# Start-up constants, early loads, transposes, filler matmuls and the last store rearranged in a fused window-attention and SwiGLU kernel

## The chip, the cores and the metric

The kernel runs on one core of one Trainium2 chip. The metric is the device time of one execution in microseconds. The median of 10 runs of the kernel before is 250.42 us (250.11 to 251.44). Five engines have their own instruction queues, each worked off in order: TensorE (PE, with its weight loads shown as PEld), VectorE (DVE), ScalarE (ACT), GpSimd (POOL) and SyncE (SP).

## The reference

Attention over a sliding window of 128 keys plus four sink tokens, for 4 batches of 8 heads with 768 positions of 64 dimensions; its output, as 3072 rows of 512, goes through RMS normalisation and a SwiGLU feed-forward network (FFN) with 1536 hidden columns.

```python
scores = scale * np.matmul(q, k.transpose(0, 1, 3, 2))
keep = is_sink | in_window            # pos < 4, or 0 <= i - j < 128
scores = np.where(keep, scores, -1000000000.0)
a = np.exp(scores - max); a = a / (sum(a) + 1e-09)
x = np.matmul(a, v)                   # to 3072 x 512
xn = x / sqrt(mean(x * x) + 1e-06) * rms_g
g = xn @ w_gate
out = (g * sigmoid(g) * (xn @ w_val)) @ w_out
```

## The kernel before, in words

**Tiling.** A block is 128 positions of one batch with all eight heads; there are 24 blocks, six a batch, numbered 0 to 23. The loop over blocks makes, for each: q and k transposed to put the head dimension on the partitions; scores of its 128 keys against its own and the next block's queries (64-row matmuls, two heads at once); exponentials on ACT; a causal and a window triangle; the attention-value product with a column of ones that gives the denominators; division; RMS normalisation; and a transpose of the normalised x. From the third block of a batch on, the sink keys enter with their own small matmuls (`ss`, `vs`). Four blocks make a group; the FFN works on six groups. An FFN unit is a `g` and a `v` part of 16 matmuls of 128 columns in group 0 (one block and four tiles of hidden columns at a time), eight of 256 in groups 1 and 2, four of 512 after that. Then the output projection `o` takes 12 matmuls for each block of 128 rows; ACT evicts it, SP stores it.

**Who sets the order.** No engine decides anything at run time. Every operation is given to a planner (class Plan) with the engines that may do it, an estimated duration, what it needs and gives, a priority and the PSUM banks it takes or drops. `Plan.run` repeatedly picks the operation that can start first, by its own estimates of engines, of DMA rings and of the eight PSUM banks, with the priority to break ties. The order it finds is then written out and is what the in-order engine queues contain. A change of any cost or priority can therefore reorder all engines.

**Loads.** q, k, v and the weights come in fp32 and are cast to bf16 on their way by DMAs that POOL issues (L327, L331, L374, L380), in the order of the string LOADS, at most eight under way (DEPTH). Only q of block 0 comes as fp32 over ACT's DMA queue, and ACT casts it (L319, L323). The gain of the normalisation, `grow`, comes over SP and is spread over the partitions by a one-row fp32 matmul `gb` (L395).

**Constants.** DVE sets tiles to a value, POOL's affine selects cut them: the identity (L253), two bias triangles (L260, L265), two mask triangles (the same lines), `sel` (L288) and `headm` (L297, L302). Blocks 0 to 2 get their triangles from PE, which adds the biases to the scores with four 512-column matmuls (L434, PE_MASKS); blocks 3 to 11 get them from DVE, by a product with the masks (L482), and later blocks from POOL (L487, L492), except the first block of a batch, which stays on DVE.

**Transposes.** q, k (L412) and x (L575) of blocks 0 to 9 are transposed by PE into PSUM and copied out by DVE or ACT (L419, L581). From block 10 on, SP issues DMA transposes from SBUF to SBUF (L426, L587); those of q and k wait for the scores of three blocks before.

**Gates.** Scores of block 8 and later wait for an FFN unit chosen by GATE_FROM and GATE_LEAD, so that attention does not run too far ahead of the FFN. SPLIT names the blocks whose scores are made in two halves, those against the own queries first.

Of the kernel before, what the change touches and what calls it, by code (L numbers as in the profile page):

```python
# [9 lines left out]
ALU = mybir.AluOpType  # L10
ACT = mybir.ActivationFunctionType
# [4 lines left out]
P = 128  # L16
# [7 lines left out]
NEG = -30000.0  # L24


class Plan:
# [21 lines left out]
    def land(self, ring, first, work):  # L49
# [3 lines left out]
        if ring == "POOL":  # L53
            r["POOL"] = max(first, r["POOL"], r["HW"]) + work
            self.loads -= 1
            return r["POOL"] + 520
# [10 lines left out]
    def run(self):  # L67
# [12 lines left out]
        while left:  # L80
# [23 lines left out]
            if e == "PE":  # L104
                busy = [(a, d) for a, d in busy if a > start - 4000]
                warm = start - free[e] < 4000 and (warm or sum(d for a, d in busy) > 2600)
                ns = ns if warm else 1.9 * ns
                if o["mode"] != mode:
                    ns, mode = ns + 110, o["mode"]
                busy.append((start, ns))  # L110
# [24 lines left out]
def kernel(  # L135
# [33 lines left out]
    F32_LOADS = ("q0",)  # L169
    POOL_AT = (0,2,6)  # L170
    DEPTH = 8
    LOADS = "k-0 v-0 qk-1 w-0-2 qkv-2 v-1 w-2-5 qkv-3 w-5-9 w-9-12 qkv-4 wo-0-6 qkv-5 wo-6-12 qkv-6 qkv-7 qkv-8"
    LOADS += "".join(f" qkv-{g}" for g in range(9, NB))
    PE_MASKS = 3
    POOL_MASK_FROM = 12
    X_DMA_FROM = 10
    QK_DMA_FROM = 10
    LD = 16
    GATE_FROM = 8
    GATE_LEAD = 2  # L180
    T_LEAD = 3
    SPLIT = (0,)
    CHUNKS = (4,2,2)
    GB_PRIO = -1200
# [35 lines left out]
    headm = const.tile([P, H], BF16, name="headm")  # L220
# [27 lines left out]
    dve(480, lambda: nc.vector.memset(masks, 1.0), gives=["masks0"], prio=-40)  # L248
    dve(70, lambda: nc.vector.memset(sel, 0.0), gives=["sel0"], prio=-39)
    dve(70, lambda: nc.vector.memset(headm, 1.0), gives=["headm0"], prio=-38)  # L250
# [7 lines left out]
    def triangle(t, fill, i):  # L258
        if i == 0:
            nc.gpsimd.affine_select(  # L260
                out=t, in_=t, compare_op=ALU.is_ge,
                fill=fill, base=0, pattern=[[1, P]], channel_multiplier=-1,
            )
        else:
            nc.gpsimd.affine_select(  # L265
                out=t, in_=t, compare_op=ALU.is_ge,
                fill=fill, base=-1, pattern=[[-1, P]], channel_multiplier=1,
            )
# [5 lines left out]
    def spread_masks():  # L274
        nc.vector.tensor_copy(out=masks[:, 0, :, :], in_=masks[:, 1, :, :])
        nc.vector.memset(masks[0:NS, 0, :, :], 1.0)

    pool(270, make_ident, ["id0"], ["ident"], -89.2 + POOL_AT[0])
    for i in range(2):
        pool(270, lambda i=i: triangle(bias[:, i, :], NEG, i), ["bias0"],  # L280
             [("bias", i)], -89.1 + POOL_AT[1] + i / 100)
# [598 lines left out]
```

## Time and profile before

| what | us |
|---|---|
| median of 10 runs | 250.42 |
| the profiled execution, own time | 250.14 |
| its span, first to last instruction | 248.4 |
| PE busy | 238.2 (96%) |
| PE weight loads busy | 148.7 (60%) |
| DVE busy | 177.7 (72%) |
| ACT busy | 133.0 (54%) |
| POOL busy | 95.2 (38%) |
| first real matmul starts | 3.97 |
| last matmul ends | 244.64 |
| issue to landing, fp32 q of block 0 | 3.0 |
| issue to landing, a 256 KB store, median | 2.2 |

Times in the profile are microseconds from the first instruction, so the span is shorter than the execution's own time by what lies around it. Matmuls overlap one another, so a busy time of PE does not tell how fast it runs; the chain of the work that ended last gives start-to-start prices. A line such as L452 is the line of the kernel. In the changed kernel most lines stand a few numbers lower or higher: L452 becomes L455, L412 L415, L434 L437, L752 L755, L785 L788.

### The profile page before, as it was taken

Reading aid. Unit: us, or ns where it says so; the run is one execution under the profiler, and the core shown is the slowest. Engines: PE = TensorE matmul, PEld = TensorE weight load, DVE = VectorE, ACT = ScalarE, POOL = GpSimd, SP = SyncE. Lnnn points to the kernel's source line nnn. Section 1 sums busy time; section 2 is a strip of 40 time slices with the busy share of each in tenths; the row PEclk is TensorE's granted clock in tenths of the full one; section 3 lists DMA queues with packets and bytes.
Section 4 is the critical chain, followed back from the end, with each engine's and each line's share of the span. In section 5 each row is a group of like instructions: output and inputs, shape, how many; then the busy total and the mean of one; then the engine's idle time right before and its main releaser. Section 6 shows DMA issues by size and latency. Waiting matters only on the chain.

```text
span 248.4 us, 5479 instructions
## 1 busy us (share of the span) xinstructions
PE 238.2 (96%) x2094; PEld 148.7 (60%) x2094; DVE 177.7 (72%) x470; ACT 133.0 (54%) x277; POOL 95.2 (38%) x129
## 2 busy tenths in 40 slices
PE   3898999999999999999999999999999999999993
PEld 1456998696689875589775445444455454444441
DVE  2376889699899996599986089997279993377700
ACT  3566466787937644645753545644645543333111
POOL 8996455599942589204403111020303320000000
PEclk9999999999999999999999999999999999999999
DMA  9999999999999999996222533212501102200022
GB/s 90 148 178 187 199 189 186 156 180 154 150 172 154 147 155 148 170 200 90 42 46 63 148 66 65 56 31 80 152 24 22 22 18 83 112 3 0 0 84 84
DMA packets 107003, 26.43 MB, mean 106 GB/s; under 512 B 98273, under 2 KB 103905, under 8 KB 106978
## 3 DMA queue, kind: packets, MB, share of 16 engines
q0 software_dynamic: 79632, 14.03, 75.6%
q1 hardware_dynamic: 26306, 11.81, 23.7%
q8 instruction: 16, 0.26, 0.5%
q10 hardware_dynamic: 1040, 0.26, 0.5%
q14 instruction: 9, 0.07, 0.1%
HBM read 28.31 MB, written 6.29 MB: 139 GB/s over the span
## 4 chain that ended last, share of the span: by engine, by line
PE 93%; DMA 2%; ACT 1%; DVE 1%; POOL 1%; issue 1%; POOLq 0%
PE o L785 25%; PE g L752 25%; PE v L752 25%; PE s L452 5%; PE av L516 3%; PE av L511 2%; DMA q<-in_q_dram 2%; PE ss L618 1%; PE av L501 1%; PE q L412 1%; PE x L575 1%; PE k L412 1%; PE gb L395 1%; PE s L434 1%; ACT e L465 1%
## 5 line engine op out<-in xcount | busy, mean ns | idle before, releaser
L752 PE MATMUL v<-xnt,wv 128*128 128x128 bf16 (+2 forms) x528 | 72.6, 282 | 0.2 <-DMA wv<-in_moe_w_val_dram 0.2
L752 PE MATMUL g<-xnt,wg 128*128 128x128 bf16 (+2 forms) x528 | 70.2, 282 | 0.1
L759 ACT ACTIVATE th<-g 128x512 bf16<-128x512 f32 x72 | 43.1, 602 | 43.4 <-PE g L752 43.3
L765 DVE SCALAR_TENSOR_TENSOR p<-th,g 128x512 bf16<-128x512 bf16 x72 | 48.1, 684 | 25.2 <-ACT th L759 24.9
L785 PE MATMUL o<-wo,hT 128*128 128x512 bf16 x288 | 66.1, 379 | 0.0
L752 PEld LDWEIGHTS <-wg 128*128 128x128 bf16 x528 | 43.1, 98 | 19.4 <-issue 1.6
L465 ACT ACTIVATE e<-s 128x512 bf16<-128x512 f32 (+1 forms) x100 | 48.4, 553 | 10.2 <-PE s L452 10.1
L752 PEld LDWEIGHTS <-wv 128*128 128x128 bf16 x528 | 42.4, 98 | 18.2 <-issue 1.1
L775 DVE TENSOR_TENSOR hT<-p,v 128x512 bf16<-128x512 bf16 x72 | 47.7, 682 | 1.8 <-PE v L752 0.8
L785 PEld LDWEIGHTS <-hT 128*128 128x128 bf16 x288 | 26.8, 97 | 30.1 <-issue 0.8
L487 POOL TENSOR_SCALAR_AFFINE_SELECT e<-e 128x512 bf16<-128x512 bf16 x20 | 13.9, 698 | 80.3 <-ACT e L465 54.0
L793 ACT ACTIVATE osb<-o 128x512 f32<-128x512 f32 x24 | 14.5, 603 | 26.1 <-PE o L785 25.9
L327 POOL DMA_DIRECT2D k<-in_k_dram x24 | 21.5, 896 | 10.1 <-DMA v<-in_v_dram 2.5
L327 POOL DMA_DIRECT2D q<-in_q_dram x23 | 20.6, 895 | 10.6 <-DMA wo<-in_moe_w_out_dram 3.0
L536 ACT ACTIVATE sq<-x 128x512 bf16<-128x512 bf16 x24 | 15.2, 633 | 17.0 <-DVE x L528 16.8
L331 POOL DMA_DIRECT2D v<-in_v_dram x24 | 21.5, 894 | 5.8 <-DMA q<-in_q_dram 4.7
L528 DVE TENSOR_TENSOR x<-av,rden 128x256 bf16<-128x256 f32 x48 | 20.4, 425 | 1.7
L560 DVE SCALAR_TENSOR_TENSOR xr<-x,r,gb 128x512 bf16<-128x512 bf16 x24 | 18.0, 752 | 0.9
L516 PE MATMUL av<-v,e 128*128 128x65 bf16 x192 | 17.1, 195 | 0.2
L452 PE MATMUL s<-qkT 64*128 64x256 bf16 (+1 forms) x200 | 14.5, 268 | 0.8 <-DVE qkT L419 0.5
L511 PE MATMUL av<-v,e 128*128 128x65 bf16 x160 | 14.8, 193 | 0.0
L516 PEld LDWEIGHTS <-e 128*128 128x128 bf16 x192 | 13.0, 99 | 2.0 <-ACT e L465 0.5
(68 smaller groups left out, 175.1 us busy)
## 6 DMA issues: line engine op xcount, KB each, us to landing
out_dram<-osb SPq DMA_DIRECT2D x24, 256.0 KB, 2.2
k<-in_k_dram POOLq DMA_DIRECT2D x24, 128.0 KB, 7.9
v<-in_v_dram POOLq DMA_DIRECT2D x24, 128.0 KB, 8.4
q<-in_q_dram POOLq DMA_DIRECT2D x23, 128.0 KB, 7.7
wo<-in_moe_w_out_dram POOLq DMA_DIRECT2D x2, 768.0 KB, 13.4
wg<-in_moe_w_gate_dram POOLq DMA_DIRECT2D x2, 384.0 KB, 9.3
wv<-in_moe_w_val_dram POOLq DMA_DIRECT2D x2, 384.0 KB, 10.4
wg<-in_moe_w_gate_dram POOLq DMA_DIRECT2D x1, 512.0 KB, 9.3
```

The lines of the kernel that those rows point to most:

```text
L327: nc.gpsimd.dma_start(out=T[name, g], in_=block_of(src, g))
L331: nc.gpsimd.dma_start(out=V16[b][:, t, :, 0:D], in_=block_of(v, g))
L452: nc.tensor.matmul(out=BANK[slot][:, j * 256 + n0 * P:j * 256 + n1 * P], lhsT=qkT[pr, 1, hp, t * P:(t + 1) * P], rhs=qkT[pr, 0, hp, (t + n ...
L465: nc.scalar.activation(out=T["e", g, u][:, 2 * hi:2 * hi + 2, n0:n1, :].rearrange("p x n c -> p x (n c)"), in_=ps.rearrange("p (j c) -> p ...
L511: nc.tensor.matmul(out=dest, lhsT=T["e", g - 1, u][:, x, 1, :], rhs=V16[b][:, t - 1, h, :], start=(t == 1), stop=False, skip_group_check=True,
L516: nc.tensor.matmul(out=dest, lhsT=T["e", g, u][:, x, 0, :], rhs=V16[b][:, t, h, :], start=(t == 0), stop=True, skip_group_check=True,)
L528: nc.vector.tensor_tensor(out=T["x16", g][:, 4 * u:4 * u + 4, :], in0=pvv[:, :, 0:D], in1=rden.unsqueeze(2).to_broadcast((P, 4, D)), op=AL ...
L752: nc.tensor.matmul(out=ps[:, i * n:(i + 1) * n], lhsT=w_sb[:, kt, ft * P:(ft + 1) * P], rhs=T["xnt", G][:, kt, cols], start=(kt == 0), sto ...
L759: nc.scalar.activation(out=T["th", key], in_=BANK[("g", key)], func=ACT.Tanh, scale=0.5,)
L765: nc.vector.scalar_tensor_tensor(out=T["p1", key], in0=T.pop(("th", key)), scalar=1.0, in1=BANK.pop(("g", key)), op0=ALU.add, op1=ALU.mult,)
L775: nc.vector.tensor_tensor(out=T[hk][:, i:i + n, cols], in0=T.pop(("p1", key)).rearrange("p (n c) -> p n c", n=n), in1=BANK.pop(("v", key)) ...
L785: nc.tensor.matmul(out=BANK[("o", G, tb)], lhsT=T["h", G, ft // 4][:, ft % 4, tb * P:(tb + 1) * P], rhs=wo[:, ft, :], start=(ft == 0), sto ...
```

## The change

- **Constants.** POOL makes the identity and one bias triangle. DVE makes the other bias as the complement of the first (with a fill of -32768), both masks from the biases by a comparison with zero, `sel` as a copy of identity columns and `headm` as a sum over them. POOL issues its first load before it makes the identity.
- **Loads.** q and k of block 0 and q of block 1 come as fp32 over SP; q0 and k0 are cast on ACT and q1 on DVE. `grow` comes over ACT. LOADS changes its order: smaller pieces of the gate and value weights, block 3 ahead of tiles 2 and 3, block 8 ahead of blocks 6 and 7. From block 9 on, a block's loads wait for the scores of nine blocks before.
- **Transposes** of q, k and x by DMA from block 8.
- **Masks.** PE adds the bias for blocks 0 to 3; POOL masks from block 14.
- **Gates.** Attention may run eight FFN units further ahead, from block 6; scores of blocks 1 and 2 are split too.
- **Fillers.** 20 matmuls of 128 columns on a tile of zeros, into a PSUM bank of their own, at the lowest priority: the planner puts them where PE is idle by its estimate. In the resulting order seven stand ahead of everything, the rest in ones to threes up to block 2's bias.
- **The last block.** Its output projection is made in two halves of 256 columns; ACT evicts and stores the first, DVE evicts and SP stores the second.
- **Planner.** Its estimates of early DMA transfers, of load latency and of when PE runs at full speed change.

The diff, cut to its core:

```diff
-NEG = -30000.0
+NEG = -32768.0
...
-            r["POOL"] = max(first, r["POOL"], r["HW"]) + work
+            begin = max(first, r["POOL"], r["HW"])
+            r["POOL"] = begin + (1.4 * work if begin < 8500 else work)
...
-                busy = [(a, d) for a, d in busy if a > start - 4000]
-                warm = start - free[e] < 4000 and (warm or sum(d for a, d in busy) > 2600)
-                ns = ns if warm else 1.9 * ns
+                busy = [(a, d) for a, d in busy if a > start - 3413]
+                warm = start - free[e] < 4000 and (warm or sum(d for a, d in busy) > 3000)
+                ns = ns if warm else 2 * ns
                 if o["mode"] != mode:
                     ns, mode = ns + 110, o["mode"]
-                busy.append((start, ns))
+                busy.append((start, ns if mode < 2 else 0))
...
-    F32_LOADS = ("q0",)
-    POOL_AT = (0,2,6)
+    F32_LOADS = ("qs0","ks0","qs1")
+    GROW = "ACT"
+    CAST_DVE = 1500
+    MASKS_PRIO = -5
+    POOL_AT = (0,1)
     DEPTH = 8
-    LOADS = "k-0 v-0 qk-1 w-0-2 qkv-2 v-1 w-2-5 qkv-3 w-5-9 w-9-12 qkv-4 wo-0-6 qkv-5 wo-6-12 qkv-6 qkv-7 qkv-8"
+    LOADS = "k-1 v-0 qkv-2 w-0-2 v-1 qkv-3 w-2-4 w-4-6 w-6-8 w-8-9 w-9-12 qkv-4 wo-0-6 qkv-5 wo-6-12 qkv-8 qkv-6 qkv-7"
     LOADS += "".join(f" qkv-{g}" for g in range(9, NB))
-    PE_MASKS = 3
-    POOL_MASK_FROM = 12
-    X_DMA_FROM = 10
-    QK_DMA_FROM = 10
+    PE_MASKS = 4
+    POOL_MASK_FROM = 14
+    X_DMA_FROM = 8
+    QK_DMA_FROM = 8
     LD = 16
-    GATE_FROM = 8
-    GATE_LEAD = 2
+    GATE_FROM = 6
+    LOAD_LEAD = 9
+    LEAD_FROM = 9
+    WARM = 20
+    GATE_LEAD = 10
     T_LEAD = 3
-    SPLIT = (0,)
+    SPLIT = (0,1,2)
     CHUNKS = (4,2,2)
-    GB_PRIO = -1200
+    GB_PRIO = 2000
...
+    if WARM:
+        zeros = const.tile([P, P], BF16, name="zeros")
+        dve(70, lambda: nc.vector.memset(zeros, 0.0), gives=["zeros"], prio=-99.6)
...
+    def make_bias():
+        nc.gpsimd.affine_select(
+            out=bias[:, 0, :], in_=bias[:, 0, :], compare_op=ALU.is_ge,
+            fill=NEG, base=0, pattern=[[1, P]], channel_multiplier=-1,
+        )
+    def other_bias():
+        nc.vector.tensor_scalar(
+            out=bias[:, 1, :], in0=bias[:, 0, :], scalar1=-1.0, scalar2=NEG,
+            op0=ALU.mult, op1=ALU.add,
+        )
...
+    def make_masks():
+        for i in range(2):
+            nc.vector.tensor_scalar(
+                out=masks[:, i], in0=bias, scalar1=0.0, scalar2=None, op0=ALU.is_equal,
+            )
         nc.vector.memset(masks[0:NS, 0, :, :], 1.0)
+    def make_sel():
+        nc.vector.tensor_copy(
+            out=sel[:, 0:H * NS].rearrange("p (h s) -> p h s", s=NS),
+            in_=ident[:, 0:NS].unsqueeze(1).to_broadcast((P, H, NS)),
+        )
+        nc.vector.reduce_sum(
+            out=headm, in_=ident[:, 0:H * NS].rearrange("p (h s) -> p h s", s=NS),
+            axis=mybir.AxisListType.X,
+        )
...
     pool(270, make_ident, ["id0"], ["ident"], -89.2 + POOL_AT[0])
-    for i in range(2):
-        pool(270, lambda i=i: triangle(bias[:, i, :], NEG, i), ["bias0"],
-             [("bias", i)], -89.1 + POOL_AT[1] + i / 100)
-        pool(330, lambda i=i: triangle(masks[:, 1, i, :], 0.0, i), ["masks0"],
-             [("masks1", i)], -89.1 + POOL_AT[2] + i / 100)
-    dve(220, cut_ident, ["ident"], ["idnos"], -50)
-    dve(600, spread_masks, [("masks1", 0), ("masks1", 1)], ["masks"], -20)
-
...
-    pool(200, make_sel, ["sel0"], ["sel"], -89.1 + POOL_AT[2] + 1)
-    pool(180, lambda: make_headm(0), ["headm0"], ["headm1"], -89.1 + POOL_AT[2] + 2)
-    pool(180, lambda: make_headm(1), ["headm1"], ["headm"], -89.1 + POOL_AT[2] + 3)
+    pool(270, make_bias, ["bias0"], [("bias", 0)], -89.1 + POOL_AT[1])
+    dve(130, other_bias, [("bias", 0)], [("bias", 1)], -60)
+    dve(220, cut_ident, ["ident"], ["idnos"], -59)
+    dve(700, make_masks, [("bias", 0), ("bias", 1)], ["masks"], MASKS_PRIO)
+    dve(300, make_sel, ["ident", "sel0"], ["sel", "headm"], MASKS_PRIO + 1)
...
-        n, g = name[0], int(name[1:])
-        src, first, fn = q if n == "q" else k, i % 2 == 0, load_f32
-        if first:
-            op({"ACT": (450, 1000, lambda n=n, src=src, g=g: load_f32(n, src, g, nc.scalar))},
-               (), [(n + "st", g)], -90 + i, ring="HW", work=970)
-        else:
-            sp(400, 1000, lambda n=n, src=src, g=g: load_f32(n, src, g, nc.sync),
-               (), [(n + "st", g)], -90 + i, ring="HW", work=970)
-        act(640, lambda n=n, g=g: cast(n, g, nc.scalar.copy), [(n + "st", g), "table"],
-            [(n, g)], -99)
-    sp(400, 1000, lambda: nc.sync.dma_start(
-        out=grow, in_=moe_rms_g.rearrange("(o d) -> o d", o=1)), (), ["grow"], -89.5, ring="HW", work=50)
+        n, g, e = name[0], int(name[2:]), {"s": "SP", "a": "ACT"}[name[1]]
+        src, eng = q if n == "q" else k, {"SP": nc.sync, "ACT": nc.scalar}[e]
+        op({e: (430, 1000, lambda n=n, src=src, g=g, eng=eng: load_f32(n, src, g, eng))},
+           (), [(n + "st", g)], -90 + i, ring="HW", work=970)
+        either({"DVE": (CAST_DVE, lambda n=n, g=g: cast(n, g, nc.vector.tensor_copy)),
+                "ACT": (640, lambda n=n, g=g: cast(n, g, nc.scalar.copy))},
+               [(n + "st", g), "table"], [(n, g)], -99)
+    op({GROW: (430, 1000, lambda: {"SP": nc.sync, "ACT": nc.scalar}[GROW].dma_start(
+        out=grow, in_=moe_rms_g.rearrange("(o d) -> o d", o=1)))}, (), ["grow"], -89.5,
+        ring="HW", work=50)
...
-        op({"POOL": (ns, 1720, fn)}, list(needs) + more, list(gives) + [("sw", n)], -89 + n,
+        op({"POOL": (ns, 1900, fn)}, list(needs) + more, list(gives) + [("sw", n)], -89 + n,
...
-        old = g - LD
         for n in what:
+            needs = [("s", g - LOAD_LEAD)] if g >= LEAD_FROM else []
             if n == "v":
-                sw_load(lambda g=g: load_v(g), [("v", g)], 910)
+                sw_load(lambda g=g: load_v(g), [("v", g)], 910, needs=needs)
             else:
                 src = q if n == "q" else k
+                needs += [(n + "T", g - LD)] if g >= LD else []
                 sw_load(lambda n=n, src=src, g=g: load_bf16(n, src, g), [(n, g)], 860,
-                        needs=[(n + "T", old)] if old >= 0 else [])
+                        needs=needs)
...
+    def warm(i):
+        ps = bank(("warm",)) if i == 0 else BANK[("warm",)]
+        nc.tensor.matmul(out=ps[:, 0:P], lhsT=zeros, rhs=zeros, start=True, stop=True)
+    for i in range(WARM):
+        pe(55, lambda i=i: warm(i), ["zeros"] + ([("warm", i - 1)] if i else []),
+           [("warm", i)], 1e9, takes=[("warm",)] if i == 0 else (),
+           drops=[("warm",)] if i == WARM - 1 else ())
...
+    def project_half(i):
+        ps = bank(("o", "last", i))
+        for ft in range(FTN):
+            nc.tensor.matmul(
+                out=ps[:, 0:DM // 2],
+                lhsT=T["h", NG - 1, ft // 4][:, ft % 4, GN - P:GN],
+                rhs=wo[:, ft, i * DM // 2:(i + 1) * DM // 2],
+                start=(ft == 0), stop=(ft == FTN - 1),
+            )
+    def evacuate_half(i):
+        T["last", i] = opool.tile([P, DM // 2], FP32, name=f"last{i}", bufs=1)
+        ps = BANK[("o", "last", i)][:, 0:DM // 2]
+        if i:
+            nc.vector.tensor_scalar(
+                out=T["last", i], in0=ps, scalar1=0.5, scalar2=None, op0=ALU.mult,
+            )
+        else:
+            nc.scalar.mul(T["last", i], ps, 0.5)
+    def store_half(i):
+        (nc.scalar if i == 0 else nc.sync).dma_start(
+            out=out[NB * P - P:NB * P, i * DM // 2:(i + 1) * DM // 2], in_=T["last", i],
+        )
...
-        for tb in range(GB):
+        for tb in range(GB if G < NG - 1 else GB - 1):
...
+    for i in range(2):
+        pe(12 * 109, lambda i=i: project_half(i), [("h", key) for key in mine]
+           + [("O", NG - 1, GB - 2)], [("ol", i)], 1e5 + i, takes=[("o", "last", i)])
+        (dve if i else act)(330, lambda i=i: evacuate_half(i), [("ol", i)], [("ev", i)],
+                            drops=[("o", "last", i)])
+        op({"SP" if i else "ACT": (420, 1000, lambda i=i: store_half(i))}, [("ev", i)], (),
+           ring="ST", work=440)
```

## The prediction

> **What bounds the kernel now.** I read the busy time by stretch first, because it tells where TensorE is not full. Columns: stretch in us, its length, then busy us (and instructions) of PE, weight loads, DVE, ACT and POOL, granted clock, DMA share, GB/s.
>
> ```profile
> 10.00:15.00 5.00, 5.00 (x35) 2.90 (x34) 2.99 (x13) 2.97 (x9) 4.99 (x8) 1.00 2.06 161
> 15.00:20.00 5.00, 4.37 (x59) 3.06 (x56) 2.64 (x9) 3.73 (x9) 3.87 (x6) 1.00 1.58 185
> 20.00:25.00 5.00, 4.10 (x60) 3.37 (x61) 3.38 (x10) 3.71 (x8) 3.47 (x4) 1.00 1.58 194
> 25.00:30.00 5.00, 5.00 (x96) 4.83 (x94) 4.05 (x14) 2.37 (x6) 1.92 (x3) 1.00 1.30 205
> 30.00:240.00 210.00, 209.89 (x1810) 130.04 (x1808) 161.77 (x410) 115.29 (x239) 71.91 (x92) 1.00 0.96 98
> ```
>
> From 25 us to the end PE idles for 0.1 us. So the end is the moment at which PE becomes full, plus the work left, plus the tail after the last matmul. The second view is the waits, of PE alone: every one of them lies before 25 us.
>
> ```profile
> PE s L434 <- POOL bias L265: 4.0, 1, 4.0
> PE q L412 <- DMA q<-in_q_dram: 0.6, 2, 0.3
> PE x L575 <- DVE xr L560: 0.5, 1, 0.5
> PE v L752 <- DMA wv<-in_moe_w_val_dram: 0.2, 1, 0.2
> ```
>
> A busy PE need not be a fast PE. Third, the timeline: four mask matmuls of 512 columns, the same instruction three times (start, us).
>
> ```profile
> 3.97 1.86 PE L434 MATMUL s<-bias,idnos 128*128 128x512 bf16 x4 [3.97 <-POOL bias L265]
> ...
> 12.48 1.91 PE L434 MATMUL s<-bias,ident 128*128 128x512 bf16 x4
> ...
> 16.18 1.04 PE L434 MATMUL s<-bias,ident 128*128 128x512 bf16 x4
> ```
>
> The granted clock says 1.00 throughout, but equal work costs 1.9 us before about 16 us and half of that after. Fourth, the chain that ended last gives the prices of the steps (start, us, step):
>
> ```profile
> 8.73 2.00 PE gb L395 x2
> ...
> 12.69 1.71 PE s L434 x4
> ...
> 33.64 0.22 PE q L412 x4
> ...
> 45.50 0.86 PE o L785 x4
> 46.72 0.33 PE s L452 x8
> 47.04 0.97 PE o L785 x4
> ...
> 244.64 0.60 ACT osb L793
> ```
>
> Prices at full speed: a 128-column transpose of four 0.22; four 512-column matmuls 0.86; a change into or out of the 64-row score matmuls 0.11 (0.97 less 0.86). With these I price everything PE has issued by 25.96 us, where it is full: 12 mask matmuls 2.6, ten transposes 2.2, scores of blocks 0 to 2 with their changes 2.4, sink work 0.7, gb 0.9, attention-value products 1.5, four FFN units of 0.89 make 3.6; 13.8 in all. The start therefore loses 25.96 - 13.8 = **12.1 us**, and only this, PE's later work, and the tail can change the time.
>
> **The change, part by part.**
>
> *PE's later work.* Blocks 8 and 9 lose q, k and x transposes on PE: 6 x 0.22 = -1.33. Block 3 gets its mask on PE (PE_MASKS 4): +0.86. Splitting the scores of blocks 1 and 2 adds one visit to the 64-row mode net: 2 x 0.11 = +0.22. The last block's 12 matmuls of 512 columns become 24 of 256; the trace's 256-column FFN units cost 0.87 for eight, the same per column: 0. Sum **-0.2**. Off PE, ACT and DVE lose six copies (0.59 or 0.42 each); DVE trades block 3's two masks (0.69 each) for those of block 13, which leave POOL; both are hidden under a full PE.
>
> *Tail.* From the last matmul, 244.64, to the end of the span, 248.43, is 3.8: an eviction of 0.60, a store of 256 KB that takes at best 2.0 from issue to landing, and the close. Now the last eviction is half as wide, on DVE (the 128x256 read from PSUM at L528 takes 0.43): -0.17. Half a store saves between 0 and 1.0 (all of it proportional); the issue (0.33) and the latency do not shrink, so I take -0.3. Sum **-0.45**.
>
> *Constants.* Six selects leave POOL (0.33, 0.33, 0.31, 0.29, 0.21, 0.21: 1.7 us of busy time). POOL issues the loads, but a load issued at 7.61 landed at 13.54, just 0.95 behind the one ahead of it: the transfers queue for some 6 us, so a faster POOL is worth nothing there. What counts is the very first load, issued at 1.47 and now ahead of the identity, about a microsecond earlier, and the first mask: it waits for one select and a DVE op instead of two selects behind two DMA issues, so PE starts near 2.5 instead of 3.97. DVE takes the rest, about 1 us, before its first copy at 6.73.
>
> [...] The cast of q1, fp32 SBUF to SBUF, goes to DVE now. [...] The row: POOL's issue of k at 8.74 took 0.92 beside a 0.42 DVE copy at 8.77 (PSUM source, so not quite the case), against a 0.88 median. [...]
>
> *Order of loads.* q0, k0 and q1 come as fp32 over SP (the old q0 took 2.98 from issue to landing); k0 and q1 landed at 5.27 and 8.08 before, and I expect 5 and 6.3. But the transfers ahead of the weights of the first FFN unit are about as many: before, nine 128 KB blocks' worth (q0, k0, v0, q1, k1, q2, k2, v2, v1) and ten 128 KB weight slices until wv of tiles 2 to 4 landed at 20.00; now these nine plus q3, k3, v3 (0.9 each, +2.7) but two slices of weights fewer (-1.3 to -1.6), with a start about 1 us earlier: wg near 18.7, wv near 20. The loads of blocks 9 on wait for scores nine blocks back. The wait holds up POOL's queue: the loads behind it, and last the block masks from block 14. By PE's order block 14's scores come near 107, so block 23's loads issue then instead of 98 to 100; block 14's masks come right after them and its attention-value product near 131, and block 23 is needed near 178. Covered; uncovered it would be the 2.7 us of four masks (about 0.67 each).
>
> *Fillers.* Twenty 128-column matmuls on zeros: seven while PE has nothing to do, 13 between real ones at 0.107 each while the clock is low (0.43 for four in the chain): 0 to 1.4 us in the way; I take 0.4, since most stand at waits.
>
> [...] I count **0** for the clock.
>
> *What the start then takes.* I walk the new order with the old durations. q0, k0, k1 transposed by 6.7; scores of block 0 at 7.2, as before; q1's at 7.7; gb until 10.1; second scores 10.2 (before 10.73); block 1's mask needs the banks that block 0's exponentials free, 12.3 (before 12.48), but its q2 and k2 are transposed ahead of it, so block 1's scores start near 14.1 instead of 15.49. Its eight half-size exponentials run at 0.30 each back to back: products of block 1 at 16.5 instead of 17.28. The new order then puts block 2's scores and block 3's transposes before the first FFN unit, so that unit starts near 19.2 (before 18.33) with 9.4 us of work behind PE instead of 7.7. Then block 2's products wait for ACT (near 20), x1 near 21, and x2, ahead of the fifth unit, near 25.0. With every exponential at 0.39 instead, ACT is 1.2 later and x2 comes at 26.4. At x2 PE has done 15.1. So the loss is 10.1 to 11.5; I take 10.7 with the fillers: **-1.4**.
>
> Sum on the profiled execution: 250.14 - 1.4 - 0.2 - 0.45 = 248.1 (its span was 248.4, so 1.7 lie around it and stay). The median of the runs stands 0.28 above this execution: **248.4**.
>
> **The rivals.**
>
> [...]
>
> *The start gains nothing.* ACT has more, smaller exponentials; fillers and x2 may cost what the earlier scores gain. For: PE's wait for xr, 0.5, is already there. Then only -0.65 is left: 249.8.
>
> *Slower: blocks 6 and 7 starve.* Their transposes on PE now run exactly when their loads land: k6 landed at 47.37 and PE used it at 48.24; q7 at 49.23, used at 49.35. The change puts q8, k8, v8 (0.9 each, 2.7) ahead of them, and block 8's two DMA transposes, about 1 us of transfer each, into the same stretch. PE's order has moved them back by about as much: k6 near 50.4, q7 52.5, k7 52.8, when loads shifted by 2.7 land at 50.1, 51.9 and 52.8. If the two transposes come on top, k7 is up to 2 late, and everything behind it on PE. In the profile, a DMA transpose in a loaded queue took up to 9.6 us against 2.4 in an empty one. For: no slack. Against: the load stream starts about a microsecond earlier. It decides from 2.0 us of stall, where the gains are gone; at 2.5 to 3 us of stall, 250.9 to 251.4.
>
> **How the numbers follow.** Chances: the forecast 0.45 (own range 247.6 to 249.2), the earlier clock 0.20, no gain at the start 0.15, starvation 0.20. A measurement of this kernel can tell about 0.2%, 0.5 us, from no change: faster means below 249.9. The first two are faster, and about 0.06 of the third, which sits at the edge; 0.06 of the third and 0.03 of the fourth are the same; the rest slower: 0.71, 0.09, 0.20. Range for 8 in 10: the earlier clock with a full tail, 246.9, to the starvation's start, 250.8; beyond it lie its longer stalls and a clock two windows early.
>
> **What would show it.** Right: PE starts near 2.5; masks of block 1 still near 1.9 for four; PE is full from about 25, with x2 transposed near 25 to 26; no PE wait for q or k of blocks 6 and 7; last matmul near 243; tail near 3.3. Wrong: a mask at half price gone by 12.5 (earlier clock); x2 later than 26.5 (no gain); PE waits on q, k or a transpose between 45 and 60, or a PE share below full after 30 (starvation). The forecast fails most easily on ACT's order in the first 25 us, which I know by durations and not by its waits.

## The result

The changed kernel takes **249.27 us** (median of 15 runs, 248.05 to 250.1); the kernel before, in the same comparison, 250.3. The ratio is **0.9954** (95% interval 0.9942 to 0.9966), so it is faster by about 1.15 us, where the forecast had 2.0. The sign and the range held; the likeliest time was 0.9 us too low. Here and below, medians are of all runs of a kernel, and ratios of its fast runs alone, those within 1.5% of its fastest.

The profiled execution of the changed kernel took 249.92 us, 0.65 above its own median; that of before took 250.14, 0.16 below its median. The two traces therefore differ by only 0.22 us, and each term below is first read on these two traces and then weighed against the medians.

The windows of the changed kernel, columns as in the prediction:

```profile
10.00:15.00 5.00, 5.00 (x36) 2.90 (x35) 2.37 (x8) 2.91 (x8) 4.53 (x6) 1.00 1.95 175
15.00:20.00 5.00, 4.76 (x63) 2.92 (x62) 3.69 (x14) 3.35 (x12) 3.71 (x5) 1.00 1.66 188
20.00:25.00 5.00, 4.71 (x74) 3.81 (x73) 4.15 (x16) 4.29 (x14) 2.94 (x4) 1.00 1.51 193
25.00:30.00 5.00, 4.84 (x88) 4.72 (x86) 3.77 (x10) 2.28 (x4) 3.72 (x5) 1.00 1.49 196
30.00:240.00 210.00, 209.45 (x1799) 129.94 (x1797) 163.45 (x412) 110.09 (x230) 68.37 (x88) 1.00 1.05 101
```

PE gains 0.39 and 0.61 between 15 and 25 us (4.37 and 4.10 before). It loses 0.16 of that from 25 to 30 and 0.44 after 30, where it had been full. PE's waits, all of them:

```profile
PE s L437 <- DVE bias L273: 1.9, 1, 1.9
PE warm L390 <- DVE zeros L258: 1.1, 1, 1.1
PE k L415 <- ACT k L318: 0.5, 1, 0.5
PE ss L621 <- DVE qkT L422: 0.3, 1, 0.3
PE av L514 <- ACT e L468: 0.2, 1, 0.2
PE v L755 <- DVE hT L778: 0.2, 1, 0.2
PE av L519 <- DVE m L546: 0.2, 1, 0.2
PE g L755 <- DVE hT L778: 0.2, 1, 0.2
```

No q, k or transpose of blocks 6 to 9 is waited for. The three waits that are new after 25 us are the last ones, for DVE's products (`hT`) and a normalisation step (`m`). The timeline of the start (start, us):

```profile
3.87 1.86 PE L437 MATMUL s<-bias,idnos 128*128 128x512 bf16 x4 [1.89 <-DVE bias L273]
...
9.22 2.07 PE L398 MATMUL gb<-grow,ones 1*128 1x512 f32 x2
14.00 1.91 PE L437 MATMUL s<-bias,ident 128*128 128x512 bf16 x4
16.83 1.03 PE L437 MATMUL s<-bias,ident 128*128 128x512 bf16 x4
...
21.18 1.07 PE L755 MATMUL g<-xnt,wg 128*128 128x128 bf16 x16
...
26.64 0.39 PE L578 MATMUL x<-ident,xr 128*128 128x128 bf16 x4
```

The first mask starts at 3.87, not 2.5; the masks of block 1 still run at half rate (1.91 for four, where block 2's take 1.03), as forecast; the first FFN unit starts at 21.18, not 19.2, and x2 at 26.64, not 25.0.

The sum on the two traces, in us: with the prediction's own count of 15.1 us of work issued ahead of x2, the start lost 26.64 - 15.1 = 11.5 instead of 12.1, **-0.6**. PE's later work was to be 0.2 less. The last matmul ended at 244.96 (244.62 before; the table's 244.64 is the start of its eviction), and the span at 248.2 (248.43), so the tail is 3.24 instead of 3.81, **-0.57**. To meet the measured -0.22, PE must have lost about **1.1 after x2**. 0.6 of it shows as idle time (0.16 and 0.44 in the windows above). The rest, some 0.5, these traces do not place; a sum that gives every instruction of a kind one price may be off by as much.

### The profile page after: what moved, and what is told of

The parts are those of the page before. It is cut to its first block, busy times and chain, and to the rows that moved or that the text cites. A ratio compares the mean times of both kernels' runs of the same rounds, so it can differ in the third digit from the quotient of the medians.

```text
span 248.2 us, 5553 instructions
## 1 busy us (share of the span) xinstructions
PE 240.3 (97%) x2122; PEld 151.5 (61%) x2122; DVE 181.2 (73%) x477; ACT 129.6 (52%) x278; POOL 92.1 (37%) x121
## 4 chain that ended last, share of the span: by engine, by line
PE 82%; DVE 11%; issue 2%; DMA 2%; ACT 2%; SPq 0%
PE v L755 23%; PE g L755 22%; PE o L788 20%; PE s L455 4%; PE av L519 2%; DMA stage<-in_k_dram 2%; DVE x L531 2%; PE ss L621 2%; DVE r L559 2%; PE av L514 1%; DVE e L485 1%; DVE hT L778 1%; PE av L504 1%; PE o_last L806 1%; PE s L437 1%
## 5 line engine op out<-in xcount | busy, mean ns | idle before, releaser
L755 PE MATMUL v<-xnt,wv 128*128 128x128 bf16 (+2 forms) x528 | 70.9, 282 | 0.3 <-DVE hT L778 0.2
L788 PE MATMUL o<-wo,hT 128*128 128x512 bf16 x276 | 65.3, 379 | 0.0
L468 ACT ACTIVATE e<-s 128x512 bf16<-128x512 f32 (+1 forms) x108 | 49.3, 526 | 12.6 <-PE s L455 11.2
L755 PEld LDWEIGHTS <-wv 128*128 128x128 bf16 x528 | 43.2, 98 | 19.7 <-issue 1.2
L788 PEld LDWEIGHTS <-hT 128*128 128x128 bf16 x276 | 25.2, 98 | 27.0 <-issue 1.7
L490 POOL TENSOR_SCALAR_AFFINE_SELECT e<-e 128x512 bf16<-128x512 bf16 x18 | 11.6, 651 | 52.4 <-ACT e L468 42.2
L322 POOL DMA_DIRECT2D k<-in_k_dram x23 | 20.4, 889 | 17.4 <-DMA v<-in_v_dram 8.5
L326 POOL DMA_DIRECT2D v<-in_v_dram x24 | 21.4, 891 | 10.1 <-DMA q<-in_q_dram 8.1
L322 POOL DMA_DIRECT2D q<-in_q_dram x22 | 19.5, 884 | 14.7 <-DMA k<-in_k_dram 5.9
L796 ACT ACTIVATE osb<-o 128x512 f32<-128x512 f32 x23 | 13.8, 601 | 19.5 <-PE o L788 19.5
## 6 DMA issues: line engine op xcount, KB each, us to landing
wo<-in_moe_w_out_dram POOLq DMA_DIRECT2D x2, 768.0 KB, 12.1
```

What stands on the lines that cost most here:

```text
L322: nc.gpsimd.dma_start(out=T[name, g], in_=block_of(src, g))
L326: nc.gpsimd.dma_start(out=V16[b][:, t, :, 0:D], in_=block_of(v, g))
L468: nc.scalar.activation(out=T["e", g, u][:, 2 * hi:2 * hi + 2, n0:n1, :].rearrange("p x n c -> p x (n c)"), in_=ps.rearrange("p (j c) -> p ...
L755: nc.tensor.matmul(out=ps[:, i * n:(i + 1) * n], lhsT=w_sb[:, kt, ft * P:(ft + 1) * P], rhs=T["xnt", G][:, kt, cols], start=(kt == 0), sto ...
L788: nc.tensor.matmul(out=BANK[("o", G, tb)], lhsT=T["h", G, ft // 4][:, ft % 4, tb * P:(tb + 1) * P], rhs=wo[:, ft, :], start=(ft == 0), sto ...
```

## The experiments

Every kernel below is an edit of the changed kernel, and its ratio is to the kernel before, run on the same chip in the same comparison (its median was between 250.26 and 250.44). "After x2" is the time between the transposes of block 2's x and the last matmul.

### The fillers

No fillers issued, with all other operations in the same order:

```diff
-        nc.tensor.matmul(out=ps[:, 0:P], lhsT=zeros, rhs=zeros, start=True, stop=True)
+        for _ in range(0):
+            nc.tensor.matmul(out=ps[:, 0:P], lhsT=zeros, rhs=zeros, start=True, stop=True)
```

> The changed kernel with none of its 20 filler matmuls issued; every other instruction stands where it stood. Theory one (the 13 fillers after block 0's mask lie on PE's path, the seven ahead of it do not, and none of them moves the clock): 13 x 0.107 us at the low clock is about 1.2 us in the changed kernel's chain before 17 us, so the time falls by 0.8 to 1.2 us, from 249.3 to 248.1 to 248.5. [...]

Measured: **247.85** (247.23 to 249.34, 6 runs), ratio 0.9909 [0.9878, 0.994], less than the theory's 248.1 to 248.5. The fillers do stand in the way. The chain of the changed kernel shows where, in the stretch of half rate (start, us, step):

```profile
7.89 0.21 PE warm L390 x2
...
8.65 0.22 PE warm L390
...
12.39 0.11 PE warm L390
...
12.71 0.11 PE warm L390
...
13.04 0.11 PE warm L390
...
14.00 0.21 PE warm L390 x2
14.21 1.71 PE s L437 x4
15.92 0.11 PE warm L390
...
16.72 0.27 PE warm L390 x3
```

The rows of `warm` add up to 1.35 us. That is an upper bound, since part of them fills a wait that would otherwise be seen. Two executions with nearly the same clock bound it better. The kernel of the later experiment on gates has no fillers, and its start has the same rows at the same rate:

```profile
13.93 1.91 PE L438 MATMUL s<-bias,ident 128*128 128x512 bf16 x4
16.32 1.04 PE L438 MATMUL s<-bias,ident 128*128 128x512 bf16 x4
...
20.84 1.07 PE L756 MATMUL g<-xnt,wg 128*128 128x128 bf16 x16
...
26.31 0.39 PE L579 MATMUL x<-ident,xr 128*128 128x128 bf16 x4
```

Its first FFN unit starts 0.34 us earlier than the changed kernel's and x2 0.33 us earlier. The pair is not quite equal: there, k of block 1 landed at 7.90 instead of 7.24, and gb started 0.46 us later. With that made good, the difference would be 0.8 at most. So I put the fillers' own price at **0.3 to 0.8 us**, an estimate; the prediction took 0.4.

The rest of the 1.4 us, 0.6 to 1.1, is the clock, as far as the trace shows. In the profiled execution without fillers, the one-row gb took 1.12 instead of 2.07 us, block 1's masks 1.91 at 12.01, and block 2's 1.04 already at 14.48:

```profile
5.00:10.00 5.00, 4.05 (x32) 1.93 (x32) 0.85 (x2) 3.39 (x8) 5.00 (x7) 1.00 2.10 166
10.00:15.00 5.00, 5.00 (x49) 2.73 (x48) 3.98 (x15) 3.44 (x10) 4.54 (x6) 0.66 1.94 175
```

PE had a window of full rate before 10 us, then about 3.4 us at half rate (an estimate: a mean granted clock of 0.66 over five microseconds, with 0.50 as the low rate, which a window further down shows), and came to full rate for good some two microseconds earlier than in the changed kernel (1.04 at 14.48, 1.03 at 16.83). By the mean granted clocks, this moment differs from execution to execution of one kernel. Of the 13 runs of this kernel and of the one below with another order of loads, five have a mean granted clock of 0.993, which is what one such half-rate window makes of a whole run (an estimate: 3.4 us at 0.50 in a span of 246); they took 247.15 to 247.98. The other eight took 247.72 to 249.55, with a median of 248.82, which is 0.45 below the changed kernel. Only one of the five has a trace, and a mean of 0.993 does not prove an early window: one run of the kernel with other gates has it too, and took 249.22.

None of the changed kernel's 16 runs has a mean below 0.999. But its fillers do not keep early windows away: the experiment with masks on POOL (below) has all of them in place, and in its trace gb is at full rate before 10 us as well (1.12).

```profile
8.57 1.12 PE L398 MATMUL gb<-grow,ones 1*128 1x512 f32 x2
```

```profile
10.00:15.00 5.00, 5.00 (x52) 3.46 (x51) 4.01 (x15) 3.28 (x11) 4.51 (x7) 0.66 1.95 174
```

Whether the fillers make such windows rarer is open.

All fillers ahead of block 0's mask, where PE is idle anyway:

```diff
-        nc.tensor.matmul(out=ps[:, 0:P], lhsT=zeros, rhs=zeros, start=True, stop=True)
+        for _ in range(24 if i == 0 else 0):
+            nc.tensor.matmul(out=ps[:, 0:P], lhsT=zeros, rhs=zeros, start=True, stop=True)
```

> The changed kernel with 24 fillers ahead of block 0's mask, where PE waits until 3.87 us anyway (24 x 0.107 = 2.6 us from 1.06), and none later. Theory one: as without fillers, 248.1 to 248.5, with block 1's masks still at 1.9 us for four. [...]

Measured: 249.02 (248.64 to 250.04, 6 runs), ratio 0.9944 [0.9924, 0.9964], above the expected range. In the profiled execution block 0's four masks, at 3.87, took 1.15 instead of 1.86, and gb 1.12 instead of 2.07, behind 24 fillers that kept PE busy from 1.06 to 3.80. It is not so in every execution: three later experiments have the same 24 fillers first, and there these masks took 1.87, 1.87 and 1.02. Then the rate fell back: block 1's masks at 11.87 took 1.91, and the granted clock in the window from 10 to 15 is 0.66.

```profile
5.00:10.00 5.00, 2.90 (x35) 1.52 (x32) 0.85 (x2) 3.43 (x9) 5.00 (x7) 1.00 2.20 174
10.00:15.00 5.00, 4.99 (x46) 2.75 (x41) 4.12 (x15) 3.21 (x10) 4.51 (x7) 0.66 1.97 174
```

Between 5 and 10 us PE is busy for only 2.90 of 5.00, where it waits 1.65 us for the cast of k and 0.46 for a copy on ACT; the low rate follows that stretch. x2 came at 24.56, two microseconds earlier than in the changed kernel, and yet the time is only 0.25 less. The gain went into a stall, in the waits after 26 us and in the chain:

```profile
PE k L416 <- DMA k<-in_k_dram: 1.5, 1, 1.5
```

```profile
43.94 9.49 DMA k<-in_k_dram
...
53.47 0.40 PE k L416 x4
```

This is the prediction's starvation rival: k of block 7, issued at 43.94 beside block 8's two DMA transposes (44.63 and 45.97), took 9.49 us to land, and PE stood for it. In the changed kernel the same load landed at 51.67, and PE came to it at 53.91: a slack of two microseconds. Two things took this slack away. PE came two microseconds earlier, and the load landed 1.8 later, because it landed behind block 8's first transpose (52.97) and not ahead of it (52.03 in the changed kernel). Without fillers PE is as early (x2 at 24.46), but the load landed at 51.97, ahead of the transpose, and the wait was only 0.3 us.

The one-row gb matmul moved behind block 0's attention-value products, with the fillers as they were, and then with the fillers first:

```diff
-    pe(864, unit_gb, ["ones", "grow", ("s", 0, 0)], ["gbm"], GB_PRIO, takes=[("gb",)], mode=2)
+    pe(864, unit_gb, ["ones", "grow", ("av", 0, 1)], ["gbm"], GB_PRIO, takes=[("gb",)], mode=2)
```

> The changed kernel with the one-row fp32 matmul that spreads the gain waiting for block 0's attention-value product, so that it stands behind block 0's second scores (the planner reorders what follows). Theory: its 2.0 us at the low clock hold up block 0's second scores, their exponentials and block 1's mask; behind them it fills a wait instead: 0.8 to 1.6 us off, 247.7 to 248.5. Rival (the loads and ACT set the pace of the start, not PE): within 0.3 us of the changed kernel, 249.0 to 249.6.

> 24 fillers ahead of block 0's mask, none later, and the one-row gb matmul moved behind block 0's attention-value products. Theory A (the one-row gb is what let the clock fall back from 10.98 to 14.40 us in the run with the fillers first): the first masks at half rate until 4 to 7 us, then full rate without a break; the four masks of block 1 take about 0.9 instead of 1.9; the first FFN unit starts near 18, and the start loses 8.5 to 9.5 us instead of 10.0. Theory B (any thin stretch lets it fall): a half-rate window between 10 and 15 us again. By both k7 of block 7 is then late (landing near 53, used near 51): PE waits 1 to 2.5 us for it between 50 and 55. Time: A 248.3 to 249.3, since the wait takes back what the clock gives; B 249 to 249.8.

Measured: 249.68 (247.79 to 251.94, 12 runs), ratio 0.9948 [0.9926, 0.9971], with gb late; **250.62** (249.81 to 252.0, 12 runs), ratio 1.0006 [0.9986, 1.0026], with both. With gb late alone, block 1's masks at 13.07 took 1.04, at full rate, and x2 came at 25.05. The start gained 1.6 us, as the theory had it, but k of block 7 then cost a wait of 1.3 us, and the time is above both ranges. With both, the time is above both ranges too, and the clock fell for longer:

```profile
5.00:10.00 5.00, 3.29 (x38) 2.04 (x36) 1.08 (x2) 3.54 (x9) 5.00 (x7) 1.00 2.17 170
10.00:15.00 5.00, 5.00 (x26) 1.95 (x20) 3.41 (x13) 3.35 (x9) 4.71 (x7) 0.50 1.95 175
15.00:20.00 5.00, 4.38 (x60) 2.88 (x59) 2.76 (x11) 3.76 (x13) 3.43 (x5) 0.82 1.64 189
```

So the one-row matmul is not needed for the clock to fall: with it out of the way, 10 to 15 us ran at 0.50. What the two kernels with fillers first share is the thin stretch from 5 to 10 us (2.90 and 3.29 busy), as the second theory has it. But that is not all either. Without fillers PE was busy for 4.05 of 5.00 there, 1 us of it with the one-row matmul, and the clock fell too. The kernel before was busy for 4.10 of 5.00 from 20 to 25 us, with no one-row matmul, and kept 1.00. Both may count; a kernel with that stretch filled was not tried.

### The loads of blocks 6, 7 and 8

q, k and v of blocks 6 and 7 ahead of block 8's, without fillers and then with the 24 fillers first:

```diff
-    LOADS = "k-1 v-0 qkv-2 w-0-2 v-1 qkv-3 w-2-4 w-4-6 w-6-8 w-8-9 w-9-12 qkv-4 wo-0-6 qkv-5 wo-6-12 qkv-8 qkv-6 qkv-7"
+    LOADS = "k-1 v-0 qkv-2 w-0-2 v-1 qkv-3 w-2-4 w-4-6 w-6-8 w-8-9 w-9-12 qkv-4 wo-0-6 qkv-5 wo-6-12 qkv-6 qkv-7 qkv-8"
```

> No fillers, and q, k, v of blocks 6 and 7 loaded ahead of those of block 8. Against the kernel without fillers alone (247.85), whose PE waited 0.3 us for k of block 7. If the order of these loads is what starves block 7: that wait is gone, k7 lands near 49 instead of 52, and the time is 247.3 to 247.7. If the DMA transposes of block 8 become late instead, PE waits for qT or kT of block 8 and the time is the same or up to 1 us more.

> 24 fillers ahead of block 0's mask, none later, and q, k, v of blocks 6 and 7 ahead of block 8's. The same with block 8 ahead took 249.02 and its PE stood 1.5 us for k of block 7. If the order of the loads is the cause of that stall (the rival called starvation): the stall is gone or under 0.3 us, and the time is 247.4 to 248.0. If block 8's DMA transposes hold up the loads whatever their order: k7 still lands near 53, and the time is 248.6 to 249.2.

Without fillers: 248.63 (247.15 to 249.55, 7 runs), ratio 0.9918 [0.9885, 0.995], against 0.9909 with block 8 ahead, so no difference that these runs can tell. k of block 7 landed at 49.22 instead of 51.97 and was not waited for, but a wait of 0.3 us was all there was to gain. In the profiled execution x2 was one microsecond later (25.46 instead of 24.46); there the early window of full rate did not come.

With the fillers first: **247.69** (246.98 to 248.9, 6 runs), ratio **0.9889** [0.9857, 0.9921], 1.3 us less than with block 8 ahead. k of block 7 now stands ahead of block 8's loads. It was issued at 39.10 instead of 43.94 and landed at 48.52 instead of 53.43. It was in flight for 9.4 us in both: what it gained is its place in the order. k of block 8, now at 44.19 where k of block 7 had been, and with no DMA transpose beside it, took 6.95 us. Of PE's waits after 26 us only one is left, 0.2 us for a product of DVE.

So the order of these loads is the cause of the 1.5 us stall, and the rival's mechanism is shown: not in the changed kernel, but in kernels whose start is faster. This is the best kernel of the study, 1.6 us below the changed one.

### DMA transposes, gates and the last block

DMA transposes from block 10 again, without fillers:

```diff
-    X_DMA_FROM = 8
-    QK_DMA_FROM = 8
+    X_DMA_FROM = 10
+    QK_DMA_FROM = 10
```

> No fillers, and the DMA transposes begin at block 10 again, so that blocks 8 and 9 are transposed on PE. By the prediction's step (six transpose groups of 0.22 leave PE, 1.33 us): 249.2, which is 1.3 more than without fillers alone. By the rival (block 8's transposes starve the loads of blocks 6 and 7, and the copies are not what DVE lacks): k7 lands 2 us earlier, its wait of 0.3 is gone, and the time is 248.5 to 248.9. If DVE and ACT are short between 55 and 70 us, six copies more (0.4 to 0.6 each) add to it: 249.5 to 250.

Measured: 249.23 (247.96 to 249.99, 12 runs), ratio 0.9944 [0.9924, 0.9963], which is 249.2 as the step has it. By the medians that is partly luck: the 247.85 that the step adds to has four of six runs below 248, and against the 248.82 of the other eight above, the difference is 0.4. Against the execution with loads reordered, whose start is nearly the same (x2 at 25.33 here and 25.46 there), the last matmul ended at 244.38 instead of 243.49. So after x2 it took 1.0 us more, for 1.33 more of work on PE. The other 0.3 came back: between 145 and 170 us, PE is full here (the row is shown below).

The gates on the scores (from block 8 on, with a lead of two, as before), without fillers. The expectation calls them gates of loads, which was a mistake of mine: GATE_FROM and GATE_LEAD hold back scores, and LOAD_LEAD holds back loads.

```diff
-    GATE_FROM = 6
+    GATE_FROM = 8
...
-    GATE_LEAD = 10
+    GATE_LEAD = 2
```

> No fillers, and the gates of the late loads as before (from block 8 on, with a lead of two). By the prediction the gates cost nothing: 247.6 to 248.1, the same as without fillers alone. If holding back the loads is what keeps the load queue free for blocks 6 to 8: blocks 9 and 10 load earlier, between 45 and 60 us, PE waits longer for k7, and the time is 248.3 to 249. If the masks of the last blocks on POOL come late because they stand behind gated loads: PE's small losses between 147 and 165 us (0.6) go, and the time is 247.3.

Measured: 248.98 (248.34 to 249.8, 11 runs), ratio 0.9942 [0.9924, 0.9959]. The expectation for unhindered loads does not apply, since no load was changed. Its runs lie near the 248.82 of the eight runs above with a mean clock near 1. It is 1.1 above the 247.85 without fillers alone, but only one of its 11 runs has a mean clock below 0.999. No effect of these gates is shown.

The last block whole, with the fillers as they were:

```diff
-        for tb in range(GB if G < NG - 1 else GB - 1):
+        for tb in range(GB):
...
-    for i in range(2):
-        pe(12 * 109, lambda i=i: project_half(i), [("h", key) for key in mine]
...
```

> The changed kernel with its last output block whole, one eviction on ACT and one store of 256 KB, as before the change. Forecast's term: 0.45 us dearer, 249.7. If the half saves only the eviction's difference (0.17): 249.4; if the store's time is proportional to its size (1.0): 250.4.

Measured: 249.67 (248.41 to 250.24, 10 runs), ratio 0.9966 [0.995, 0.9982] against 0.9954. The difference of 0.0012 is 0.3 us, and the intervals overlap. In the traces the tail is 3.24 instead of 3.81. The forecast's 0.45 lies between the two. The last store took 1.70 us from issue to landing instead of 2.02, and the last eviction 0.43 instead of 0.60.

### The masks that moved to DVE

After 145 us PE is no longer full, beside a DVE that nearly is. The same window of the kernel before:

```profile
145.00:170.00 25.00, 25.00 (x172) 11.98 (x169) 23.22 (x59) 13.43 (x29) 3.63 (x6) 1.00 0.21 39
```

and of the changed kernel:

```profile
145.00:170.00 25.00, 24.64 (x159) 11.78 (x158) 24.32 (x54) 12.59 (x26) 5.25 (x8) 1.00 0.27 58
```

DVE is busy for 1.1 us more, and PE for 0.36 less. One wait of PE shows:

```profile
162.50 1.02 PE L755 MATMUL v<-xnt,wv 128*128 128x512 bf16 x4 [0.22 <-DVE hT L778]
```

The two expectations below take the mask products at 145.65 and 148.64 for block 13's, which the change moves from POOL to DVE. That was a misreading. They are the last two of DVE's 22 and belong to block 18, which is the first of a batch and has its masks on DVE in both kernels (at 159.87 and 163.79 before). Block 13's are these, in a stretch where PE is full (75.00 of 75.00 us between 70 and 145):

```profile
102.82 0.69 DVE L485 TENSOR_TENSOR e<-e,masks 128x1024 bf16<-128x1024 bf16 x1
...
103.98 0.68 DVE L485 TENSOR_TENSOR e<-e,masks 128x1024 bf16<-128x1024 bf16 x1
```

To move block 13's masks back to POOL, one constant:

```diff
-    POOL_MASK_FROM = 14
+    POOL_MASK_FROM = 12
```

> The changed kernel with one constant back: the block masks go to POOL from block 12 again, so that block 13's two (0.68 each) leave DVE at 145 to 149 us. The prediction held them to be hidden under a full PE. If that is so: 249.2, the same as the changed kernel. If they are what fills DVE between 145 and 165 us and what PE loses there (about 0.65 us in the changed kernel and in the one without fillers): DVE has slack between 145 and 165 again, PE is full there, and the time is 0.5 to 0.7 less, 248.5 to 248.8. If POOL, with its gated loads, now brings block 13's masks late: PE waits for them near 145 and the time is over 249.3.

> No fillers, blocks 6 and 7 loaded ahead of 8, block masks on POOL from block 12. The first two edits alone took 248.63 (247.15 to 249.55). If the terms add: about 0.6 less, 247.8 to 248.1, with no loss of PE after 30 us. If the losses between 145 and 165 us are of another cause: 248.4 to 248.8.

Measured: **253.88** (250.93 to 257.94, 12 runs), ratio 1.0072 [1.004, 1.0105], and without fillers and with the loads reordered **254.6** (252.8 to 256.5, 6 runs), ratio 1.0164 [1.0119, 1.0208]. By the ratios the constant costs 3.0 and 6.2 us. The first of the two was traced in one of its longer executions, 255.48. PE's largest wait there:

```profile
PE av L519 <- POOL e L490: 4.5, 1, 4.5
```

In the second, traced at 252.8, PE waited 3.1 us for POOL's masks. POOL's timeline in the first:

```profile
104.64 0.88 POOL L322 DMA_DIRECT2D q<-in_q_dram  x1 [0.18 <-issue]
106.84 0.87 POOL L322 DMA_DIRECT2D k<-in_k_dram  x1 [1.33 <-DMA v<-in_v_dram]
107.72 0.65 POOL L490 TENSOR_SCALAR_AFFINE_SELECT e<-e 128x512 bf16<-128x512 bf16 x1
```

Block 13's masks stand in POOL's queue behind loads, and each load waits for the landing of the one eight before it. In the kernel before, the last load was issued at 100.14 and the first of these masks at 113.23, after 12.20 us in which POOL had nothing to do. In the changed order PE comes to these masks near 104 (it stood 4.5 us, until 108.4), and loads are issued until 117.87. So block 13's masks could not have stayed on POOL beside the rest of the change.

What costs PE the 0.36 between 145 and 170 stays open. Block 13's masks do not lie there. A DVE that is nearly full is not enough: with gb late, DVE was busy for 21.84 there, less than before, and PE still lost 0.43. And with the DMA transposes from block 10, and the same masks on DVE, PE lost nothing:

```profile
145.00:170.00 25.00, 25.00 (x163) 11.96 (x162) 23.02 (x56) 13.03 (x26) 5.25 (x8) 1.00 0.25 53
```

Is it the new wait of the loads for scores nine blocks before that makes them late? Without it, with the fastest start and order of loads:

```diff
-    POOL_MASK_FROM = 14
+    POOL_MASK_FROM = 12
...
-    LEAD_FROM = 9
+    LEAD_FROM = 99
```

> 24 fillers first, blocks 6 and 7 loaded ahead of 8, block masks on POOL from block 12, and the loads no longer waiting for scores nine blocks back. The same start with masks from 14 and the waiting loads took 247.69. If the wait for scores is what put the loads, and behind them POOL's masks of block 12, too late (PE stood 3.1 to 4.5 us for them): the last load of block 23 is issued near 100 instead of 112 to 118, the wait is gone, DVE has slack from 145 to 165, and the time is 246.9 to 247.3. If the loads are held up by the DMA transposes of blocks 8 and 9 and by the depth of eight loads in flight instead: the last load is still issued after 108, PE waits 2 us or more for POOL's masks near 105, and the time is over 250.

Measured: **257.74** (255.27 to 259.63, 6 runs), ratio 1.0282 [1.0238, 1.0326]. The signs of the second theory came: PE waited 7.5 us for POOL's masks, 5.6 of it at once, and the last load was still issued at 115.31. The gate alone is not the cause. The limit of eight loads shows in the releasers below; the share of the DMA transposes was not tried by itself. POOL's timeline, with the landing of the load eight before as the releaser:

```profile
106.10 0.87 POOL L322 DMA_DIRECT2D k<-in_k_dram  x1 [2.96 <-DMA v<-in_v_dram]
106.98 0.65 POOL L491 TENSOR_SCALAR_AFFINE_SELECT e<-e 128x512 bf16<-128x512 bf16 x1
```

The loads landed 10 to 17 us after their issue there (before: 6.4 to 7.6 for those issued from 86 to 96 us). With eight under way, that lets POOL issue one every 1.2 to 2 us (an estimate: these times over eight).

## Why the prediction was right, and where it was off

**What was right.** The sign, the range, and the chance put on faster. In the trace, block 1's masks kept the half rate (1.91 for four at 14.00), as the row of before said (1.91 at 12.48). There is some luck in that, since an execution with the same fillers had the early window (gb 1.12 at 8.57). The fillers' price (0.4 taken, 0.3 to 0.8 by the traces), the tail (0.45 taken, 0.57 in the traces, 0.3 in the medians) and the DMA transposes (1.33 of PE's work, of which 1.0 is found at the end in the traces and 0.4 in the medians) were about of the right size. Nothing starved. The load issued at 7.90, under the cast of q1 at 8.01, took 1.03 against a median of 0.89: 0.14 late, where the prediction's row was 0.04 late (0.92 against 0.88).

**"What the start then takes", -1.4, was mis-sized.** It measured about -0.6 in the profiled pair, and -0.4 if one counts as the prediction's own range does (it gives 10.1 for x2 at 25.0, where 25.0 - 15.1 is 9.9; its seven prices, too, add up to 13.9 and not 13.8). The step that failed first is in "Order of loads" and in the walk's "q0, k0, k1 transposed by 6.7". k0 and q1 were expected at 5 and 6.3 and landed at 6.05 and 7.99. The one row to go by was q0 alone, 2.98 us from issue to landing. Now q0 took 3.31, k0 4.73 and q1 6.05, each issued beside the ones before it. k1, the first load of POOL, was issued at 1.31 and landed at 7.24, and PE's order has its transposes ahead of block 0's scores. So these scores came at 8.10, not 7.2. From there each step is late: gb ends at 11.29 instead of 10.1, block 1's masks start at 14.0 instead of 12.3, block 1's scores at 15.96 instead of 14.1, the first FFN unit at 21.18 instead of 19.2. Fillers are part of this: the chain has 0.97 us of them by 14.21. The expected first mask at 2.5 failed too: POOL issued its first load at 1.31, the complement on DVE took 0.59 us, and PE started at 3.87. Little was lost by that, because PE then waits for k0 anyway.

**PE did not stay full after x2, which the prediction put at 0.** The masks of block 13 are hidden under a full PE, as it said. But PE lost 0.16 us between 25 and 30, 0.19 between 30 and 70 and 0.36 between 145 and 170 (0.11 in all before), and some 0.5 more that the traces do not place. The prediction weighed DVE's work against PE's busy time as a whole (161.77 of 210), where the windows from 145 to 170 have DVE 93% full before and 97% after. The waits that show are for products and a normalisation step of DVE. Which part of the change put them late is open.

**Starvation did not decide, for a reason I had not given.** I held it off with an earlier load stream. What saved k of block 7 was PE's late start and a landing just ahead of block 8's first transpose. In three kernels with a faster start the stall was 0.3, 1.3 and 1.5 us, within what that rival described.

**The clock as a term.** The sum counts it at 0; an earlier clock stands only in the chances (0.20) and in the range's lower end (246.9), and no run of the changed kernel shows it. What the runs showed in its place: before, PE was busy for 5.00 of 5.00 us from 10 to 15, and the masks at 12.48 still took 1.91; block 2's masks came to full rate at 16.83 (1.03) in the changed kernel's trace and at 14.48 (1.04) in the one without fillers. The runs without fillers differ by 2 us (247.23 to 249.34), in good part for the clock, as far as their mean clocks of 0.993 and 1.000 tell. This is probably also why the profiled execution shows less gain than the medians: in the one with the last block whole, whose fillers are the same, block 1's masks took 1.53 and x2 came at 26.18, 0.46 earlier. It is a reason, too, why the split of the missing 0.9 us between the start and PE's later losses is not better than about 0.3 us.

## What to carry to other kernels

Time that a faster start frees can be spent at the next place without slack (with the fillers first, 1.5 us of two, for k of block 7): ask of each load or copy that is just in time now what it would be if PE came two microseconds earlier, and move it first. Fill idle time of PE ahead of the first real work, not between real work; the same matmuls cost nothing there (block 0's masks start at 3.87 with seven fillers or 24) and 0.3 to 0.8 us, an estimate, here. When an engine issues loads with a limit on those under way, work that is queued behind them inherits their landing times (in the last experiment block 13's masks stood behind a load that POOL issued at 106.10, after 2.96 us of waiting for a landing), so masks that PE will wait for belong on it only after the last load.

## What the runs showed of the hardware

One stall of PE stands beside a loss longer than itself. In the last experiment PE waited 7.5 us, and the granted clock fell to 0.81 and 0.85 there (the windows of that kernel; the clock is the column after POOL's busy time):

```profile
100.00:110.00 10.00, 4.42 (x31) 2.68 (x30) 3.32 (x13) 2.02 (x6) 5.32 (x8) 0.81 1.60 201
110.00:120.00 10.00, 8.12 (x69) 6.36 (x68) 5.04 (x11) 4.14 (x9) 3.66 (x6) 0.85 2.03 162
```

Between 100 and 120 us PE is short of 7.46 us of busy time. The kernel took 10 us more than the one with the same start, the masks of block 13 on DVE and the waiting loads (257.74 and 247.69), for 7.5 us of waiting; how much of the rest is the clock was not taken apart. The second surprise is that at the start of one execution the full rate came, went and came back within 11 microseconds (masks at 1.15 for four at 3.87 us, at 1.91 at 11.87 us, at 1.04 at 14.57 us in the run with the fillers first), and that in one and the same kernel its moment seems to move from run to run (mean granted clocks of 0.993 in three of the six runs without fillers, of 1.000 in the other three).
